# The first half of a weight load as four strided groups of partitions

## Chip, cores, metric

The kernel runs on one core of a Trainium2 chip. The metric is the device time of one execution in microseconds (us). Before the change it is 189.69 us, the median of six runs, one of them slow. Runs in the chip's slower state (here 193.02 us) are kept out of every ratio below, though not out of the medians.

## The reference

Two branches on a normalized input are added to the input. Branch A is attention for one new token per sequence over the last 4096 entries of a key and value cache; branch B is a small dense layer. Cut to what matters here:

```python
xn = layernorm(x)                      # 2 sequences, 448 features
q = xn @ wq                            # wq: 448 x 4096
k, v = last 4096 rows of the caches    # 2 x 8 heads x 4096 x 256, bf16
o = softmax(q k^T / 16) v
out = x + o @ wo + mish(xn @ w1 + b1) @ w2
```

The work is nearly all reading: 77.7 MB come from HBM, of which wq is 3.67 MB.

## The kernel before

All loads but two small ones (5.3 KB, from ScalarE's queue) are issued by SyncE, on one queue. wq is the first of them. It is laid out as 128 partitions of seven steps of 2048 elements, and comes in two transfers: four steps (16 KB for each partition), then three (12 KB).

```python
wq_sb = v_tile()[:, 0 : NS * HW].rearrange("p (s n) -> p s n", s=NS)      # NS = 7, HW = 2048
wq_in = A_wq.rearrange("r (x n) -> (r x) n", x=NX).rearrange("(p s) n -> p s n", s=NS)
SC = NS // 2 + 1                                                          # 4
for lo, hi in ((0, SC), (SC, NS)):
    nc.sync.dma_start(out=wq_sb[:, lo:hi, :], in_=wq_in[:, lo:hi, :])
# ... layer norm, masks, constants
load_k(0)          # 4 MB of K: the second thing on the queue
load_dense()       # w1, w2
project()          # q = xn @ wq: 28 matmuls, s outermost, so the first 16 need only the first half
build_q(0); build_q(1)
turn(0)            # VectorE transposes a piece of K; scores() needs it and q
# ... loop over heads: load_k(i + 1), load_v(i), load_wo(i), scores, values
```

The softmax here doesn't subtract the row's maximum and nothing guards it: scores larger than these inputs give would overflow.

## Time and profile before

| | before |
|---|---|
| median of 6 runs | 189.69 us (189.51 to 193.02) |
| span of the profiled run | 187.9 us |
| bytes on SyncE's queue, share of 16 engines | 77.66 MB, 96.8% |
| PE / DVE busy | 81% / 57% |
| first data, first K transpose | 1.7 us, 21.48 us |

The span is from the first to the last instruction; the time is some 1.75 us longer. A DMA share of 1.00 means that all 16 DMA engines are at work. The lines themselves stand in the prediction. One more is needed for later, the stretch from 4 to 12 us, with the DMA share and GB/s as its last two columns:

```profile
4.00:12.00 8.00, 4.78 (x19) 1.91 (x20) 3.31 (x19) 0.00 (x0) 0.05 (x1) 1.00 1.02 435
```

It is at the steady rate of the whole run: after the ramp of the first microseconds, wq is read as fast as anything else (435 GB/s against 428 to 432 in the stretches from 20 to 160 us).

### The profile page before, as it was taken

The numbers are of one execution on the slowest core, as the hardware profiler recorded it, in microseconds if no ns is written. First come the engines' busy times: TensorE is split into PE (matmuls) and PEld (weight loads), VectorE is DVE, ScalarE is ACT, GpSimd is POOL, SyncE is SP. The second block draws the span as 40 slices with busy tenths as digits, with TensorE's granted clock in tenths as the row PEclk, the third lists the DMA queues.
The fourth block names the chain that finished last, engine by engine and source line by source line (L and its number), as shares of the span: only waits on it lengthen the run. The fifth ranks groups of instructions, "written<-read, shape, count | busy, mean of one in ns | idle before, by whom it ended". The sixth has DMA issues, their size and how long they took to land.

```text
span 187.9 us, 2493 instructions
## 1 busy us (share of the span) xinstructions
PE 151.5 (81%) x981; PEld 74.0 (39%) x981; DVE 106.9 (57%) x144; ACT 45.4 (24%) x148; POOL 16.5 (9%) x74
## 2 busy tenths in 40 slices
PE   0494099904989999979996999968995999999892
PEld 0141033901334364425342354434441534464781
DVE  5505497049671994089704991099506983976311
ACT  3005015200062225123322124033402223125101
POOL 7001500300003000200030003000110000000000
PEclk9999559965799999999999699999998799999955
DMA  6999899999999999999999999999999999999990
GB/s 224 420 474 446 376 434 439 439 443 446 433 446 419 406 407 436 446 439 393 472 445 440 412 426 412 440 446 418 451 433 439 394 436 419 443 439 415 412 381 27
DMA packets 5028, 77.81 MB, mean 414 GB/s; under 512 B 533, under 2 KB 1049, under 8 KB 2330
## 3 DMA queue, kind: packets, MB, share of 16 engines
q1 hardware_dynamic: 5012, 77.66, 96.8%
q8 instruction: 7, 0.11, 0.2%
q14 instruction: 3, 0.02, 0.0%
q10 hardware_dynamic: 6, 0.01, 0.0%
HBM read 77.67 MB, written 0.00 MB: 413 GB/s over the span
## 4 chain that ended last, share of the span: by engine, by line
DMA 67%; DVE 16%; PE 12%; SPq 2%; ACT 1%; issue 1%; ACTq 0%; DVEq 0%
DMA k<-in_A_k_cache_dram 57%; DVE kt L404 13%; DMA wo<-in_A_wo_dram 9%; PE sc L416 7%; PE o L477 4%; DVE pT L442 2%; SPq L373 1%; PE q L516 1%; ACT p L430 1%; PE psE L220 0%; SPq L114 0%; SPq L398 0%; PE psA L237 0%; DVE sums L451 0%; DVE osum L536 0%
## 5 line engine op out<-in xcount | busy, mean ns | idle before, releaser
L404 DVE STREAM_TRANSPOSE kt<-k 128x2048 f32<-128x2048 f32 x32 | 73.1, 2289 | 52.6 <-DMA k<-in_A_k_cache_dram 52.6
L416 PE MATMUL sc<-kt,qdiag 128*128 128x512 bf16 x256 | 65.2, 404 | 16.6 <-DVE kt L404 16.2
L430 ACT ACTIVATE p<-sc,off 128x256 bf16<-128x256 f32 x64 | 33.1, 544 | 70.9 <-PE sc L416 70.2
L416 PEld LDWEIGHTS <-qdiag 128*128 128x128 bf16 x256 | 23.8, 100 | 53.7 <-issue 23.5
L477 PE MATMUL o<-v,pT 128*8 128x512 bf16 x192 | 42.5, 379 | 0.0
L477 PEld LDWEIGHTS <-pT 128*8 128x8 bf16 x192 | 17.2, 92 | 22.4
L442 DVE STREAM_TRANSPOSE pT<-p 128x512 bf16<-128x512 bf16 x32 | 21.8, 681 | 5.8 <-ACT p L430 5.8
L289 POOL COPY qdiag<-qt 32x16 bf16<-32x16 bf16 x64 | 13.0, 249 | 120.0 <-PE sc L416 104.3
L486 ACT COPY o_sb<-o 8x512 f32<-8x512 f32 x12 | 6.3, 573 | 36.3 <-PE o L477 36.3
L516 PEld LDWEIGHTS q<-ident_f,o_sb 8*128 8x128 f32 x96 | 11.1, 186 | 3.1 <-issue 3.1
L430 ACT ACTIVATION_READ_ACCUMULATOR p<-sc,off 128x1 f32 x64 | 11.7, 183 | 0.0
L516 PE MATMUL q<-ident_f,o_sb 8*128 8x4 f32 x96 | 11.7, 249 | 0.0
L220 PE MATMUL psE<-v,act_bf 128*2 128x448 bf16 x14 | 4.9, 534 | 6.7 <-DVE act_bf L354 6.7
L269 PE MATMUL q_ps<-v,xq 128*128 128x512 bf16 x28 | 7.8, 446 | 2.5 <-DMA v<-in_A_wq_dram 2.5
L558 PEld LDWEIGHTS <-v 128*128 128x128 bf16 x256 | 7.4, 101 | 0.2 <-DMA v<-in_A_v_cache_dram 0.2
L558 PE MATMUL q<-pT,v 128*128 128x4 bf16 x256 | 7.4, 169 | 0.1
L220 PE MATMUL psE<-wo,oTm 128*2 128x448 bf16 x24 | 5.5, 352 | 1.4 <-DVE oTm L543 1.4
L269 PEld LDWEIGHTS <-xq 128*128 128x128 bf16 x28 | 3.1, 111 | 7.2 <-DVE xq L260 2.5
L279 DVE CAST q_sb<-q_ps 128x512 bf16<-128x512 f32 x2 | 1.3, 686 | 7.7 <-PE q_ps L269 7.7
L220 PEld LDWEIGHTS <-act_bf 128*2 128x2 bf16 x14 | 1.6, 117 | 9.7 <-DVE act_bf L354 6.8
L190 PE MATMUL xnT_ps<-ident,xn_bf 2*128 2x2 bf16 x7 | 0.5, 166 | 4.7 <-DVE xn_bf L138 4.7
L279 ACT CAST q_sb<-q_ps 128x512 bf16<-128x512 f32 x2 | 1.1, 589 | 12.0 <-PE q_ps L269 12.0
(62 smaller groups left out, 45.0 us busy)
## 6 DMA issues: line engine op xcount, KB each, us to landing
k<-in_A_k_cache_dram SPq DMA_DIRECT2D x7, 4096.0 KB, 27.3
v<-in_A_v_cache_dram SPq DMA_DIRECT2D x7, 4096.0 KB, 29.2
k<-in_A_k_cache_dram SPq DMA_DIRECT2D x2, 2048.0 KB, 24.6
v<-in_B_w_dram SPq DMA_DIRECT2D x2, 1568.0 KB, 24.5
wo<-in_A_wo_dram SPq DMA_DIRECT2D x7, 448.0 KB, 30.5
v<-in_A_wq_dram SPq DMA_DIRECT2D x1, 2048.0 KB, 7.4
v<-in_A_v_cache_dram SPq DMA_DIRECT2D x1, 2048.0 KB, 14.9
v<-in_A_wq_dram SPq DMA_DIRECT2D x1, 1536.0 KB
```

The lines of the kernel that those rows point to most:

```text
L220: nc.tensor.matmul(psE[:], lhsT=lhsT, rhs=w, start=start, stop=stop, skip_group_check=True)
L269: nc.tensor.matmul(ps[u][:], lhsT=xq[:, s, :, :].rearrange("p j k -> p (j k)"), rhs=wq_sb[:, s, u * N5 : (u + 1) * N5], start=(s == 0), st ...
L279: copy(out=q_sb[:, u * N5 : (u + 1) * N5], in_=ps[u][:])
L289: nc.gpsimd.tensor_copy(out=tv[rows, :, e, j * Q : (j + 1) * Q : HS].rearrange("p n (b h) -> p n b h", b=Bsz), in_=qv[rows, :, h0 : h0 + r ...
L404: nc.vector.transpose(out=kt[:].bitcast(FP32), in_=k[:, half * TH * Dh : (half + 1) * TH * Dh].bitcast(FP32),)
L416: nc.tensor.matmul(psc[:], lhsT=qdiag[i % NW][:, n * NE + e, :], rhs=ktv[:, n, e, :, :], start=(n == 0 and e == 0), stop=(n == NB - 1 and ...
L430: nc.scalar.activation(out=pv[:, b, :, :], in_=sv[:, b, :, :], func=ACT.Exp, scale=scale, bias=off[:, b : b + 1], accum_out=state["rs", i] ...
L442: nc.vector.transpose(out=pT[:], in_=p_t.pop(s)[:])
L477: nc.tensor.matmul(po[:], lhsT=pT_t[i * NH + piece][:, uh * NP * Q : (uh + 1) * NP * Q : HS], rhs=v[:, u * NP : (u + 1) * NP, :].rearrange ...
L486: nc.scalar.copy(out=o_sb[:, u, :, :, :], in_=po[:, u * Dh : (u + 1) * Dh] .rearrange("r (m j) -> r j m", j=NJ) .unsqueeze(2) .to_broadcas ...
L516: nc.tensor.matmul(pqv[:, j, :], lhsT=o_sb[:, u, j, :, :].rearrange("r h m -> r (h m)"), rhs=ident_f[0:NR, u * BR : (u + 1) * BR], start=( ...
L558: nc.tensor.matmul(po[:, c, :], lhsT=vv[:, t, c, :], rhs=pTv[:, th, 0:Q:HS], start=(t == 0 and c == 0), stop=(t == T - 1), skip_group_chec ...
```

## The change

Intent, as far as the diff shows: let all 16 DMA engines begin sooner. The first transfer becomes four, of 16, 16, 32 and 64 rows of the same 16 KB, on every eighth partition from 0, every eighth from 4, every fourth from 2 and every second from 1. Together they are the same 128 rows.

```diff
-    for lo, hi in ((0, SC), (SC, NS)):
-        nc.sync.dma_start(out=wq_sb[:, lo:hi, :], in_=wq_in[:, lo:hi, :])
+    for g, step in ((0, 8), (4, 8), (2, 4), (1, 2)):
+        nc.sync.dma_start(out=wq_sb[g:P:step, 0:SC, :], in_=wq_in[g:P:step, 0:SC, :])
+    nc.sync.dma_start(out=wq_sb[:, SC:NS, :], in_=wq_in[:, SC:NS, :])
```

## The prediction

Rival A is a gain of the start alone. Step 4 and the rivals B and C suppose that the rows of strided transfers slow one another, in part (B) or throughout (C). By how much was the author's estimate; no trace of the kernel before shows it.

> **What bounds the kernel now.** I read the page top down: the slices first, then the DMA queues, then the chain that ended last, and after that I opened the first microseconds, because the change touches only the first transfer of the program.
>
> ```profile
> DMA  6999899999999999999999999999999999999990
> GB/s 224 420 474 446 376 434 439 439 443 446 433 446 419 406 407 436 446 439 393 472 445 440 412 426 412 440 446 418 451 433 439 394 436 419 443 439 415 412 381 27
> ...
> q1 hardware_dynamic: 5012, 77.66, 96.8%
> ...
> DMA 67%; DVE 16%; PE 12%; SPq 2%; ACT 1%; issue 1%; ACTq 0%; DVEq 0%
> ```
>
> The reader is to see that the 16 DMA engines are full in every slice but the first and the last, and that one queue, the one SyncE issues to, moves 77.66 MB in 96.8% of the span. PE's 81% and DVE's 57% are not the limit. The chain of waits says the same: two thirds of it is loads in flight. The issues-to-landing list shows why the DMA never starves: a 4096 KB load takes 27.3 us (median) to land although 4.19 MB at about 430 GB/s is only 9.8 us of data, so some 17 us of other loads stand ahead of it when it is issued. The stretches confirm it:
>
> ```profile
> 1.60:4.00 2.40, 0.00 (x0) 0.00 (x0) 1.86 (x6) 1.56 (x2) 2.40 (x3) 1.00 0.93 315
> ...
> 20.00:60.00 40.00, 28.58 (x154) 13.77 (x154) 23.04 (x22) 8.84 (x33) 4.83 (x24) 0.77 1.01 432
> 60.00:120.00 60.00, 55.50 (x269) 25.70 (x268) 36.15 (x42) 16.06 (x54) 4.93 (x24) 0.97 1.00 429
> 120.00:160.00 40.00, 35.15 (x169) 16.23 (x168) 26.17 (x29) 10.71 (x36) 1.65 (x8) 0.96 1.00 428
> ```
>
> The last two columns are the DMA share and GB/s. The steady rate is 429 GB/s, so 26.8 GB/s for each engine, and the share is 1.00. So the time is: first data, plus 77.66 MB at 429 GB/s (181.0 us), plus what the ramp loses, plus the tail behind the last landing. A microsecond lost or won in the first transfer arrives whole at the end, since nothing later has DMA idle time to absorb it; the compute engines wait for the loads and shift with them.
>
> Now the start, in slices of 0.2 us (last column GB/s, a packet's bytes counted where it starts):
>
> ```profile
> 1.40:1.60 0.20, 0.00 (x0) 0.00 (x0) 0.20 (x1) 0.02 (x1) 0.20 (x2) 1.00 0.00 0
> 1.60:1.80 0.20, 0.00 (x0) 0.00 (x0) 0.20 (x1) 0.20 (x1) 0.20 (x1) 1.00 1.21 250
> 1.80:2.00 0.20, 0.00 (x0) 0.00 (x0) 0.20 (x1) 0.20 (x1) 0.20 (x1) 1.00 2.03 410
> 2.00:2.20 0.20, 0.00 (x0) 0.00 (x0) 0.20 (x1) 0.20 (x1) 0.20 (x1) 1.00 0.59 168
> 2.20:2.40 0.20, 0.00 (x0) 0.00 (x0) 0.17 (x2) 0.20 (x1) 0.20 (x2) 1.00 0.77 246
> 2.40:2.60 0.20, 0.00 (x0) 0.00 (x0) 0.12 (x1) 0.20 (x1) 0.20 (x1) 1.00 0.00 0
> 2.60:2.80 0.20, 0.00 (x0) 0.00 (x0) 0.20 (x1) 0.20 (x1) 0.20 (x1) 1.00 0.58 246
> ```
>
> Data begins between 1.6 and 1.8 us, and the stream is ragged for about a microsecond. Over 1.6 to 4.0 us it moved 315 x 2.4 = 756 KB, where 429 x 2.4 would be 1030 KB: 274 KB short, 0.64 us. About 0.1 us of that lies before the first packet, so at most some 0.5 us of ramp is there to be won. And the use of the tile:
>
> ```profile
> 0.73 0.87 SPq L114 DMA_DIRECT2D v<-in_A_wq_dram  x2
> ...
> 7.49 0.21 DVE L260 COPY xq<-xs 128x112 bf16<-128x112 bf16 x1
> ...
> 8.18 7.80 PE L269 MATMUL q_ps<-v,xq 128*128 128x512 bf16 x28 [2.51 <-DMA v<-in_A_wq_dram]
> ...
> 19.80 0.10 PEld L416 LDWEIGHTS <-qdiag 128*128 128x128 bf16 x1 [4.32 <-POOL qdiag L289]
> 21.48 6.70 DVE L404 STREAM_TRANSPOSE kt<-k 128x2048 f32<-128x2048 f32 x3 [3.48 <-DMA k<-in_A_k_cache_dram]
> 23.85 2.72 PE L416 MATMUL sc<-kt,qdiag 128*128 128x512 bf16 x6 [7.87 <-DVE kt L404]
> ```
>
> The projection starts when the first half of wq lands, but its result is ready (the first qdiag weight load) at 19.80, while the scores start at 23.85, behind the first K transpose at 21.48. So q has 4.05 us of slack: getting wq earlier to TensorE is worth nothing by itself. The only route from this change to the end is the DMA stream.
>
> [...]
>
> **The change part by part.**
> Removed: one 2 MiB transfer, 128 rows of 16 KiB, eight per engine. At 26.8 GB/s a row is 16.384/26.8 = 0.61 us and the eight are 4.9 us.
> Added: the same 2 MiB as 16 + 16 + 32 + 64 rows, so 1 + 1 + 2 + 4 = 8 rows per engine. Bytes, row size and order against all later loads are as before; nothing is removed from the stream.
> 1. Three more issues on SyncE. The two wq issues took 0.87 us, so 0.43 each: +1.3 us before the first K issue, which goes from 1.65 to about 2.95 us. The five wq transfers hold the engines until about 1.7 + 3.67/0.429 = 10.3 us, so all of it is hidden. The first row (0.61 us) outlasts the 0.43 us between two issues, so the small leading transfers shouldn't leave a hole. Cost 0.
> 2. Three more completions per engine and three more semaphore waits for TensorE and SyncE, each some 0.05 us going by the "issue" pieces in the chain; in q's slack of 4 us and in the backlog. Cost 0.
> 3. The ramp. [...] Of the 0.5 us above I give it 0.35 us.
> 4. [...]
> Sum: -0.35 [...].
>
> **The rivals.**
> A. Ramp gain alone [...]: 189.76 - 0.35 = 189.4 us. For it: [...] the pattern of the change looks made for the ramp. Chance 0.5.
> B. [...] about 191.8 us. [...] Chance 0.35.
> C. [...] 194.3 us. [...] Chance 0.15.
> D. The layer norm chain slips: the input's two rows, now landing by 2.48 us, could stand behind a first wq row and come 0.6 us later, moving xq from 7.70 to 8.3 us. That eats slack of q and moves the end by 0.
> E. The V load that reuses wq's buffer is issued at 16.01 us, after the projection; even 5 us later it meets a queue whose 15.3 MB, issued by 3.97 us, last to about 1.7 + 35.6 = 37 us. No effect.
>
> **Range and chances.** The weights give 0.5 x 189.4 + 0.35 x 191.8 + 0.15 x 194.3 = 191.0 as a mean, and the middle of the distribution lies at the upper edge of A. I choose 190.2 us between them. The range 189.0 to 193.9 leaves out the end of C and a gain above 0.75 us, more than the ramp holds. Faster by over 2% (below 185.96) would need 3.8 us out of a stream with 0.5 us to give: 0.01. Slower by over 2% (above 193.56) is C and the top of B: 0.14. Within 2%: 0.85.
>
> **What would show it.** Right for step 1: the first K issue near 3 us and DMA share near 1.0 from 2 to 10 us. Right for A: slices from 1.6 to 4.0 us above 315 GB/s, the projection starting at or a little before 8.18 us, K landing some 0.3 us before 21.46. Right for B or C: 200 to 350 GB/s from 2 to 10 us, the projection starting at 10 to 13 us, the first K transpose 2 to 5 us late, and all later issues late by the same, with 429 GB/s from 20 us on. Wrong altogether: a first K transpose at 21.5 us and yet another end time, which would mean that rows dealt to the engines early change the stream or the tail later; or a hole in the DMA between the wq issues, which would mean that small transfers don't keep the queue fed.

## The result, and the profile after

The changed kernel takes 191.68 us (median of six, 190.76 to 194.53, the last a slow run). A ratio here is the mean time of one kernel's fast runs over that of the other's of the same rounds, so it isn't quite the ratio of the medians. It is 1.0095, with a 95% interval of 1.0069 to 1.0122. A second set of runs, told below, gave 1.0080. So the change costs 1.5 to 1.8 us, a slowdown of under 1%.

The page of the changed kernel, its slices, queue and chain:

```profile
DMA  5999999999999999999999999999999999999990
GB/s 164 375 454 444 388 421 488 402 433 430 430 444 444 432 416 454 411 437 404 469 406 432 437 430 437 444 437 407 450 437 423 403 433 420 454 437 402 418 384 38
...
q1 hardware_dynamic: 5060, 77.66, 96.7%
...
DMA 56%; PE 23%; DVE 17%; SPq 2%; ACT 1%; issue 1%; ACTq 0%; DVEq 0%
```

Only the first two slices are poorer (164 and 375 GB/s against 224 and 420). Bytes and share are as before; 48 packets more are the completions of three more transfers on 16 engines. The chain names PE more often than before at the end, but TensorE is late there because K is. The stretches:

```profile
1.60:4.00 2.40, 0.00 (x0) 0.00 (x0) 2.40 (x3) 1.25 (x1) 2.40 (x3) 1.00 0.87 241
4.00:12.00 8.00, 2.66 (x13) 1.03 (x14) 3.83 (x24) 0.29 (x1) 0.02 (x1) 1.00 0.97 383
...
60.00:120.00 60.00, 55.85 (x271) 26.09 (x270) 36.26 (x42) 16.48 (x56) 5.82 (x29) 0.97 1.00 430
```

From 1.6 to 4 us the stream makes 241 GB/s instead of 315, from 4 to 12 us 383 instead of 435, and later 430 as before. Note the share: 0.97 of the engines are busy while only 383 GB/s flow. For the most part engines are not idle, they are slow. The start in slices of 0.2 us:

```profile
1.60:1.80 0.20, 0.00 (x0) 0.00 (x0) 0.20 (x1) 0.20 (x1) 0.20 (x1) 1.00 0.03 9
1.80:2.00 0.20, 0.00 (x0) 0.00 (x0) 0.20 (x1) 0.20 (x1) 0.20 (x1) 1.00 0.00 0
2.00:2.20 0.20, 0.00 (x0) 0.00 (x0) 0.20 (x2) 0.20 (x1) 0.20 (x1) 1.00 1.24 328
2.20:2.40 0.20, 0.00 (x0) 0.00 (x0) 0.20 (x2) 0.20 (x1) 0.20 (x2) 1.00 1.56 410
```

The first wq data come 0.4 us later than before, which no step of the prediction had. The order of events:

```profile
0.73 2.52 SPq L115 DMA_DIRECT2D v<-in_A_wq_dram  x4
...
3.29 0.60 SPq L116 DMA_DIRECT2D v<-in_A_wq_dram  x1
3.93 0.58 SPq L375 DMA_DIRECT2D k<-in_A_k_cache_dram  x1
...
10.29 7.69 PE L271 MATMUL q_ps<-v,xq 128*128 128x512 bf16 x28 [3.65 <-DMA v<-in_A_wq_dram]
...
21.79 0.10 PEld L418 LDWEIGHTS <-qdiag 128*128 128x128 bf16 x1 [4.30 <-POOL qdiag L291]
23.47 4.50 DVE L406 STREAM_TRANSPOSE kt<-k 128x2048 f32<-128x2048 f32 x2 [3.46 <-DMA k<-in_A_k_cache_dram]
```

Each wq issue takes 0.6 us (2.52 for four, gaps included), not 0.43. The projection begins at 10.29 instead of 8.18 us and the first K transpose at 23.47 instead of 21.48. So the first K load lands 2.0 us late, yet the end is only 1.1 us late in this pair of profiles (spans 187.9 and 189.0).

The trace's list of DMA packets, of which the page shows only sums, clears that up. A packet of wq's first half is one row of one partition. The 128 rows, sixteen at a time in order of their start, with the mean time of one in us; an undisturbed row takes 0.611. These tables, and the times of single rows below, are worked out from that list; no view of the page prints them:

```
rows            1-16   17-32  33-48  49-64  65-80  81-96  97-112
before          1.03   0.63   0.63   0.61   0.65   0.61   0.61
after           0.87   0.97   0.95   0.71   0.69   0.65   0.64
transfer (after) 1st    2nd    3rd    3rd    4th    4th    4th

mean lateness of the 16 engines' completions, after minus before, us:
second half of wq 1.21    first K load 1.21    last load of the program 1.28
spread of the 16 completions of the first K load: before 20.45 to 21.10, after 21.64 to 23.14
```

A load counts as landed when its slowest engine is done: the first K transpose starts 0.38 us after the last of the 16 completions before (21.10 to 21.48), and 0.33 us after it here (23.14 to 23.47). On the mean the stream is 1.21 us late at wq's second half, and it is still 1.28 us late at the last load: nothing is absorbed. The first K load looks later, by 2.0 us, because the engines are spread over 1.5 us instead of 0.65. The kernel before spreads too as it goes on (its completions near 60 us lie 1.8 us apart), so that part is no loss at the end. The five fast spans of the changed kernel average 189.2 us, against 187.95 for the fast runs of the kernel before (187.7 to 188.5): +1.25, the stream's lateness. The rest of the 1.5 to 1.8 us lies outside the span: time minus span is 1.9 to 2.9 us here and mostly 1.7 to 1.9 before. It goes with one thing in the packet lists: in three of the fourteen profiled runs an instruction load (16 or 8 KB, on the instruction queues) starts 1.8 to 2.1 us after the last instruction, and these three (the change, the change again, 32 + 32 + 64 rows) are the only ones with 2.3 to 2.9 us between span and time; the other eleven have 1.7 to 1.9. That this load is the cause, and why it comes more often here, is not shown.

Of the 1.21 us, the mean start of the 16 first rows is 0.29 later (2.41 against 2.12 us), and the rows take 0.75 longer in sum for each engine: -0.16 in the first sixteen, +0.34 in the second, +0.31 in the third, and some 0.25 in the rest. The remaining 0.17 are gaps between packets and slow rows of wq's second half.

### The profile page after: what moved, and what is told of

Its sections match the earlier page's. It is cut to its first block, busy times and chain, and to the rows that moved or that the text cites.

```text
span 189.0 us, 2498 instructions
## 1 busy us (share of the span) xinstructions
PE 151.9 (80%) x981; PEld 74.4 (39%) x981; DVE 108.0 (57%) x144; ACT 45.4 (24%) x148; POOL 16.4 (9%) x74
## 4 chain that ended last, share of the span: by engine, by line
DMA 56%; PE 23%; DVE 17%; SPq 2%; ACT 1%; issue 1%; ACTq 0%; DVEq 0%
DMA k<-in_A_k_cache_dram 56%; DVE kt L406 13%; PE sc L418 10%; PE o L479 4%; PE q L560 4%; DVE pT L444 2%; PE q L518 2%; PE psE L222 2%; SPq L115 1%; PE psA L239 1%; ACT p L432 1%; PE den L460 0%; DVE early L251 0%; SPq L116 0%; DVE sums L453 0%
## 5 line engine op out<-in xcount | busy, mean ns | idle before, releaser
L518 PEld LDWEIGHTS q<-ident_f,o_sb 8*128 8x128 f32 x96 | 11.7, 195 | 3.4 <-issue 3.4
L518 PE MATMUL q<-ident_f,o_sb 8*128 8x4 f32 x96 | 12.2, 255 | 0.0
```

The source lines that it names most:

```text
L518: nc.tensor.matmul(pqv[:, j, :], lhsT=o_sb[:, u, j, :, :].rearrange("r h m -> r (h m)"), rhs=ident_f[0:NR, u * BR : (u + 1) * BR], start=( ...
```

## The experiments

Two theories stood at the start. PORT: rows of a transfer that lies on only part of the 128 partitions slow one another and so take longer, in contiguous blocks more than at a stride. How that would come about is not shown by any trace; what the runs test is how long the rows take. ISSUE: more and longer issues on SyncE, or small transfers as such, cost the time. The edits are against the kernel before unless a line says otherwise. The four of the first set, and the four of the second (the change again among them), ran with five rounds on one chip each, beside the kernel before (189.74 and 189.79 us); the last four ran on a third chip, beside 189.85 us.

### Columns instead of partitions

```diff
+    wq_f = wq_sb.rearrange("p s n -> p (s n)"); wi_f = wq_in.rearrange("p s n -> p (s n)")
+    C = SC * HW
+    for lo, hi in ((0, C // 8), (C // 8, C // 4), (C // 4, C // 2), (C // 2, C)):
+        nc.sync.dma_start(out=wq_f[:, lo:hi], in_=wi_f[:, lo:hi])
```

> Same four sizes (256, 256, 512, 1024 KB) and the same five wq issues, but the first half of wq is cut by columns, so each transfer has all 128 partitions. PORT theory [...]: [...] DMA rate from 4 to 12 us back at about 430 GB/s, first K transpose at 21.2 to 21.8 us, time 189.4 to 190.2 us. ISSUE theory (more and longer issues on SyncE, later first data, small transfers): first K transpose still at 23 us or later, time 191 us or more.

Measured: 191.86 us, ratio 1.0120 (1.0090 to 1.0149). PORT expected no loss, and that failed. The figure is the one of ISSUE, but its cause, later first data, is not there. The stretch from 4 to 8 us:

```profile
4.00:8.00 4.00, 1.27 (x9) 0.54 (x10) 3.24 (x19) 0.00 (x0) 0.05 (x1) 1.00 0.90 282
```

The share is 0.90, and the packets show only 10 to 12 of the 16 engines at work from 3.6 to 5.6 us: holes, and from 5.2 us on single packets of 1.0 to 1.5 us where 0.15 to 0.31 would do. The holes begin where 2 KB rows give way to 4 KB rows. The start itself was the best of all: all 16 engines began between 1.74 and 2.02 us, against 1.75 to 2.77 before. So this run did not isolate what it was meant to. It says that four transfers can lose as much without any stride, in another way, and it forbids the conclusion "the loss of the change is slow strided rows, because nothing else changed".

### Contiguous blocks of partitions

```diff
+    for lo, hi in ((0, 16), (16, 32), (32, 64), (64, P)):
+        nc.sync.dma_start(out=wq_sb[lo:hi, 0:SC, :], in_=wq_in[lo:hi, 0:SC, :])
```

> Same four sizes and 16+16+32+64 rows, but contiguous partition blocks 0-15, 16-31, 32-63, 64-127. [...] PORT theory: worse than the change, [...] first K transpose 25 to 29 us, time 193 to 197 us. STRIDE theory (partitions far apart, or the HBM reads 229 KB apart, cost by themselves): no stride left, time 189.5 to 190.3 us. ISSUE theory: as the change, 191.4 us.

Measured: 195.49 us, ratio 1.0331 (1.0289 to 1.0372). From 4 to 12 us:

```profile
4.00:8.00 4.00, 0.95 (x8) 0.41 (x8) 3.26 (x20) 0.29 (x1) 0.02 (x1) 1.00 0.87 152
8.00:12.00 4.00, 0.00 (x0) 0.00 (x0) 0.57 (x5) 0.00 (x0) 0.00 (x0) 1.00 1.09 229
```

Half the steady 429 GB/s would be 214. The rows of the 64-partition block take 1.14 us (the first sixteen) and then 1.25 to 1.29, 2.1 times 0.61, with every engine busy; those of the second 16-row block 1.9. The stream ends 5.98 us late, the mean span is 6.1 us longer, and the mean time 6.3. This is the slowing that PORT expected, with no stride at all; STRIDE and ISSUE expected 191.4 us at most. It also shows lateness at the start reaching the end whole.

### Every second partition, two transfers

```diff
+    for g in range(2):
+        nc.sync.dma_start(out=wq_sb[g:P:2, 0:SC, :], in_=wq_in[g:P:2, 0:SC, :])
```

> Two transfers of every second partition (64 rows each), one issue more than before instead of three more. PORT theory: [...] the loss stays: first K transpose 22.5 to 24.5 us, time 190.8 to 192.5 us. ISSUE theory: a third of the loss, time about 190.2 us.

Measured: 190.16 us, ratio 1.0024 (1.0010 to 1.0038). PORT as first put expected 190.8 or more. ISSUE expected 190.2 and hit it, and the later first data that it named are there. Its other half, that the number of issues costs, falls in the run with the first K load in four, below.

```profile
4.00:8.00 4.00, 0.95 (x8) 0.40 (x8) 3.26 (x20) 0.29 (x1) 0.02 (x1) 1.00 1.00 423
```

Full rate, and rows of 0.61 to 0.66 us from the second on. Sixty-four strided rows did not slow each other here as the 64 contiguous ones did (1.25 to 1.29 us). The stream is 0.23 us late at the end; the first data come at 2.07 us, 0.32 later than before, and the stream shows no other loss.

### All seven steps in the four strided transfers

```diff
+    for g, step in ((0, 8), (4, 8), (2, 4), (1, 2)):
+        nc.sync.dma_start(out=wq_sb[g:P:step, :, :], in_=wq_in[g:P:step, :, :])
```

> The four strided transfers carry all seven steps (rows of 28 KB, 3.67 MB in all) and no fifth transfer follows: one issue fewer than the change. PORT theory [...]: the loss grows by less than the bytes (by 1.75 at most), time 191.3 to 192.8 us. PORT [...]: loss proportional or more, 193 us and above. ISSUE theory: a little under the change, 191 us.

Measured: 191.43 us, ratio 1.0089 (1.0076 to 1.0102), in the lower of PORT's two ranges and 0.4 above ISSUE. Longer rows (28 KB, 1.06 us undisturbed) make it plain which transfers are slow:

```
rows         1-16   17-32  33-48  49-64  65-80  81-96  97-112 113-128
us           1.92   2.02   1.56   1.06   1.06   1.06   1.06   1.06
transfer     1st    2nd    3rd    3rd    4th    4th    4th    4th
```

The two 16-row transfers run at little over half speed, 1.92 and 2.02 us against 1.06 (the first of them is slowed by the start in any case: 1.03 us instead of 0.61 for the first sixteen rows of the kernel before). The 32-row transfer is slow in its first row (1.56) and then clean; the 64-row one is clean throughout (1.06). That gave a sharper theory, SIXTEEN: only in the 16-row transfers, on every eighth partition, do rows slow one another.

### The two 16-row transfers merged

```diff
+    for g, step in ((0, 4), (2, 4), (1, 2)):
+        nc.sync.dma_start(out=wq_sb[g:P:step, 0:SC, :], in_=wq_in[g:P:step, 0:SC, :])
```

> The change with its two 16-row transfers merged into one of every fourth partition (32 + 32 + 64 rows, four wq issues, all strided). [...] SIXTEEN theory: row times fall to 0.61 us from the second row on, first K transpose at 21.6 to 22.0 us, time 189.9 to 190.5 us, the remaining loss being the later first data of a strided transfer. ALL-STRIDED theory [...]: still about 191.3 us.

Measured: 191.33 us, ratio 1.0077 (1.0057 to 1.0098). SIXTEEN was right on the rows and wrong on the time. Rows 17 to 64 took 0.62 to 0.64 us, clean, where the change has 0.97, 0.95 and 0.71. But in the third transfer (64 rows) rows 65-80 took 0.92 on the mean, up to 2.05 for a single one, and rows 97-112 took 0.86. Six engines fall behind at 5.3 us, as the third transfer begins. From 5.2 us:

```profile
5.20:5.60 0.40, 0.18 (x1) 0.10 (x1) 0.40 (x2) 0.00 (x0) 0.00 (x0) 1.00 2.05 574
5.60:6.00 0.40, 0.13 (x5) 0.13 (x5) 0.37 (x3) 0.00 (x0) 0.00 (x0) 1.00 0.76 287
6.00:6.40 0.40, 0.40 (x7) 0.18 (x5) 0.33 (x3) 0.00 (x0) 0.00 (x0) 1.00 0.63 246
```

So a second loss, of the size of the one removed, took its place. At that moment SyncE was issuing the second K load, its eighth, in 1.11 us instead of 0.55.

### The changed kernel again

The edit is the change itself.

> The changed kernel once more, on the chip of its variants: 191.2 to 191.8 us, rows of the second transfer near 1.0 us.

Measured: 191.52 us, ratio 1.0080 (1.0053 to 1.0106); rows 17-32 took 1.00 us. The rows repeat the first profile's, within 0.07 us in each group.

### Eight transfers of every eighth partition

```diff
+    for g in range(8):
+        nc.sync.dma_start(out=wq_sb[g:P:8, 0:SC, :], in_=wq_in[g:P:8, 0:SC, :])
```

> Eight transfers of every eighth partition, 16 rows each; [...]. SIXTEEN theory: [...] rows of 1.0 to 1.22 us to the end of the first half of wq, stream 3.5 to 5 us late, time 193.2 to 195.2 us. If the loss of the change came from its first microsecond only (start, ramp) [...]: about 191.5 us.

Measured: 194.38 us, ratio 1.0241 (1.0223 to 1.0259), as SIXTEEN said. The stream ends 4.78 us late.

```profile
4.00:8.00 4.00, 0.95 (x8) 0.41 (x8) 3.25 (x19) 0.00 (x0) 0.06 (x1) 1.00 1.05 225
8.00:12.00 4.00, 0.00 (x0) 0.00 (x0) 0.00 (x0) 0.00 (x0) 0.00 (x0) 1.00 0.96 198
```

Half the steady rate with all engines busy, and rows of 1.27 us (rows 33 to 64 and 97 to 128), 2.08 times the undisturbed one. At row 65, where the transfers from partitions 0 to 3 give way to those from 4 to 7, they dip to 1.08. Why they do, and why the second row of the change gets off lighter (0.97), is not shown.

A rival is the reading side: with every eighth partition, rows lie 229 KB apart in HBM. No run moves that alone. But the blocks run reads rows 28 KB apart and comes to the same 1.29 us, and the kernel before reads them 28 KB apart at 0.61. So the distance of the reads alone does not explain both slow runs. It is the partitions that tell slow rows from fast ones here: every eighth (1.27) and 64 in a block (1.29) against all 128 (0.61) and every second (0.61 to 0.66). Why these sets are slow, no run shows.

### Whole steps, no stride

```diff
-    for lo, hi in ((0, SC), (SC, NS)):
+    for lo, hi in ((0, 1), (1, SC), (SC, NS)):
```

> No strided partitions: the first half of wq as one step (128 rows of 4 KB) and three steps (12 KB), then the second half as before. A version meant to win the ramp that the change was after: in the columns run all 16 engines began within 0.3 us instead of 1.0. RAMP theory: stream 0.3 to 0.5 us earlier, time 189.2 to 189.6 us. If splitting by columns leaves holes in the DMA as the columns run did between 3.2 and 5.6 us: 190 us or more.

Measured: 189.61 us, ratio 0.9986 (0.9970 to 1.0002). The 16 engines begin between 1.74 and 2.09 us, where the kernel before has 1.75 to 2.77. But the small rows of the first transfer take longer than their share of bytes (0.54 us for the first sixteen, of 4 KB), and the stream ends 0.05 us later than before, where RAMP expected it 0.3 to 0.5 earlier. The interval includes 1, so this is not shown to be faster.

### The second K load held back

This is the run with 32 + 32 + 64 rows, and the second K load waits for a value that exists only after the projection.

```diff
     k_t[i] = k_pool.tile([P, T * Dh], BF16, tag="k", name="k")
+    if i == 1:
+        nc.vector.tensor_copy(out=k_t[i][:, 0:2], in_=qt[:, 0:2])
```

> The run with 32 + 32 + 64 rows, with the second K load held back until the projection is done, so SyncE issues seven loads in the first 5 us, as in the parity run, and not eight. In the run before it, the rows were clean up to 5.2 us and then, while that K load was being issued (1.11 us instead of 0.55), several engines took 1 to 2 us for a row. AHEAD theory (the stall comes from the eighth load being issued so early): rows near 0.61 us throughout, first K transpose at 21.6 to 22.2 us, time 189.9 to 190.5 us. If the stall is a matter of the three strided transfers themselves: first K transpose still near 23 us, time about 191.3 us. The held load meets a queue that lasts to about 26 us, so holding it costs nothing by itself.

Measured: 191.13 us, ratio 1.0076 (1.0061 to 1.0090). The load was held until 25.14 us, later than meant, since VectorE reached the copy only behind the first K transpose. The stall is there again at 5.2 us (14.2 to 15.1 of 16 engines busy until 6.4 us, single rows up to 1.46 us), though somewhat lighter: the stream ends 0.81 us late instead of 1.21. AHEAD, the theory that the eighth early issue makes the stall, falls.

### The first K load in four

```diff
-    load_k(0)
+    load_k(0, (0, T // 4, T // 2, 3 * T // 4, T))
```

> The kernel before with its first K load cut by columns into four, so nine loads are issued ahead in the first microseconds, all of 128 partitions and none strided. AHEAD theory: some engines stall for a row or more between 3 and 8 us, an issue takes over 1 us, time 190.5 to 191.8 us. If the stall needs strided partitions: 189.5 to 190.0 us.

Measured: 189.61 us, ratio 0.9991 (0.9978 to 1.0005). Three more transfers of all 128 partitions cost nothing, and no row stalls after the first. One difference to what was meant: SyncE itself waited from 4.87 to 8.44 us before the w2 load, so seven loads, not nine, had been issued in the first microseconds. AHEAD falls by the run above; this one only says that three more issues on SyncE, not strided, cost nothing here (ratio 0.9991).

### One extra load on every eighth, and on every seventh partition

```diff
+    pad = k_pool.tile([P, T * Dh], BF16, tag="k", name="pad")
+    pad_in = A_k_cache[0, 0, 0:1024, :].rearrange("(p t) d -> p (t d)", p=16)
+    nc.sync.dma_start(out=pad[0:P:8, 0 : T * Dh], in_=pad_in)        # or pad[0:112:7, ...]
```

> The kernel before with one extra load of 16 rows of 32 KB ahead of wq, on every eighth partition. PORT theory: [...] each of the 16 packets takes 2.0 to 2.4 us against 1.21 us for such a packet alone, the start included.

> The same 16 rows of 32 KB on every seventh partition (0 to 105). [...] PORT theory: about 12 packets of 1.2 to 1.6 us and 4 of 2.0 to 2.4 us. If stride or row count costs by itself, all 16 as in the run with step 8.

Measured, one look each, state unknown: 191.72 and 191.58 us. The 16 packets of 32 KB took 1.80 to 2.22 us with step 8, as expected, but 1.52 to 2.19 us with step 7, where twelve of 1.2 to 1.6 had been expected; four were below 1.6. The pair doesn't separate. It was a poor design: a first packet is slowed by the start itself (up to 1.48 us for a 16 KB row in the kernel before), as much as by its partitions. Both had their first data late, at 2.14 and 2.16 us.

## Why the prediction was right or wrong

The time fell in the range, 189.0 to 193.9, and within 2%, as the prediction held likeliest. The chosen 190.2 was too low by about 1.3 us, since it leaned on rival A. As foreseen for B and C, the first K transpose came 2.0 us late, the projection began at 10.29 us, and the rate from 20 us on was the old one.

- **The bound.** Right. The stream is late by 1.21 us at wq's second half and by 1.28 at the last load; 5.98 us in the run with blocks became 6.3 in the time. The slack of q held: its weights are ready at 21.79 us and K's transpose starts only at 23.47.
- **Step 1, three more issues, "Cost 0".** The first K issue, predicted at 2.95 us, came at 3.93, and was hidden as predicted. The step failed at the other end: a strided first transfer took 0.62 us to issue, not 0.40, and the first packet came at 2.06 to 2.16 us in all nine strided profiles, against 1.73 to 1.75 in the five whose first transfer was not strided. On the mean over engines that is 0.29 us here. Three more issues by themselves cost nothing (first K load in four: 189.61 us beside 189.85).
- **Step 2, completions and waits, 0.** Nothing speaks against it: the K load in four added three of each at no cost.
- **Step 3, the ramp, 0.35 gained.** Mis-sized. The first rows took 0.87 us instead of 1.03, so 0.16 was won, and the later start (0.29) took back more. Nor did a first transfer of 16 rows, rather than 128, set the engines off together: the sixteen starts are spread over 0.82 us here and over 1.02 before, but over 0.28 and 0.35 with 128 rows of 2 and 4 KB (columns, whole steps). The cheap way to that ramp has no stride (whole steps: all engines begin by 2.09 instead of 2.77 us), and even that did not end earlier.
- **Step 4, slow strided rows.** Right for the 16-row transfers: 1.27 us for a row where eight of them follow one another, about 1.0 in the change. Wrong for the 32- and 64-row transfers, which it took to be slow too: 64 rows ran at 0.61 to 0.66 us each (every second partition) and 1.06 us for 28 KB (all steps), and 32 rows at 0.62 to 0.64 (the merged run, from the second row on), so no slowing by the stride shows in them.
- **The sum.** B and C stood 2.0 and 4.5 us above the 189.76 us of the kernel before (191.8 and 194.3), both estimates. Measured: +1.25 in the span, +1.5 to 1.8 in the time. Rival B, "about 191.8 us", was nearest in figure and half right in cause: slow rows, for the 16-row transfers alone, plus a late start that B did not have. That its figure came so near is partly luck: slower rows were worth only 0.9 us (0.34, 0.31 and 0.25), and the late start (0.29) and the time behind the last instruction made up for much of the rest.
- **Rival D.** The transposed input came at 8.67 instead of 7.70 us in the first profile after the change, but not in the second, and in the K-in-four run too; the end didn't follow it.

What stays open: SIXTEEN accounts for the slow second row of the change, but taking the 16-row transfers out did not bring the time back. With 32 + 32 + 64 rows some engines stall as the third transfer begins. The stall is not the eighth issue on SyncE (it stayed when that was held back), and not 64 strided rows as such (the parity and all-steps runs are clean). The columns run has a stall of the same look without any stride, so the stall is not a matter of strided partitions alone. Whether the slow third row of the change (0.95 us) is slow as its second is, or by this stall, isn't separated either.

## What to carry to other kernels

Where one queue of loads sets the end, judge a cut of a transfer by the time of its rows and by the time of its first data, not by its count of issues: the rows of eight transfers on every eighth partition took 1.27 us, those of a contiguous half 1.25 to 1.29, with all 16 engines busy, against 0.61, and the loss arrived whole at the end (5.98 us in the blocks run, 6.3 in its time). If a load must be cut by partitions, 64 rows on every second partition kept the full rate here (423 GB/s), while 16 rows on every eighth (198 to 225), and a contiguous half or less (152 to 229), did not; a cut across columns or steps keeps all 128 partitions but has to be measured as well: it cost 1.2% in the columns run and nothing in the whole-steps run. And after undoing the suspected part, look at the time again: here another loss of the same size was behind it.
